# Key loads as one list of rows, scores read every third column

## The chip, the cores and the metric

The kernel runs on one core of one Trainium2 chip. The metric is the device time of one execution in microseconds; the median of several runs is compared. A core has a matrix engine (PE, with its weight loads shown apart as PEld), a vector engine (DVE), a scalar engine (ACT), a general one (POOL) and a queue engine (SP) that issues the transfers. On-chip memory (SBUF) has 128 partitions; PE writes its results to PSUM, eight banks in each partition.

## The reference

Attention of a block of 112 queries over a cache of 512 keys, with the projections before and after it, for 8 batch rows and 32 heads of 192 elements; all inputs are bf16.

```python
B, Sq, D = 8, 112, 640
H, Sk, Dh = 32, 512, 192
q = (x @ wq).reshape(B, Sq, H, Dh).transpose(0, 2, 1, 3)
scores = einsum("bhqd,bhkd->bhqk", q, k_cache) * Dh ** -0.5
p = softmax(scores, axis=-1)
o = einsum("bhqk,bhkd->bhqd", p, v_cache)
out = o.transpose(0, 2, 1, 3).reshape(B, Sq, H * Dh) @ wo
```

## The kernel before, in words

**Tiling.** The heads are taken in two halves of 16. A *group* `t` (0 to 15) is one half of the heads of one batch row: `half, b = divmod(t, 8)`. A *step* `n` (0 to 63) is four heads of a group: `t, s = divmod(n, 4)`. In each step PE computes the scores of four heads, and beside them, for earlier or later steps, the queries' projection (L313), the transposes of the probabilities (L431), the products with the values (L459, L470) and the output projection (L504). DVE takes the scaled scores out of PSUM with their row minimum (`smax`, L396), ACT takes the exponential (`exp`, L401), DVE normalises (`norm`, L405). Two buffers `s_sb` lie between `smax` and `exp`; eight buffers `p_sb` hold probabilities.

**Keys on chip.** TensorE contracts over partitions, so the 192 elements of a key must lie on partitions. Four consecutive keys are 768 elements, six pieces of 128. With `q=4` in `load_k`, a head's keys are 128 rows of 768 elements, and the transposing load (L150) of 16 heads at once sends piece number `3 a + m` of row `r` to column `r` of `kt[t % 2][:, a, m, head]`. For each head and `a` (0 or 1), `m = 0` holds elements 0 to 127 of the even key `4 r + 2 a`; `m = 1` the rest of that key in its first 64 partitions and elements 0 to 63 of the odd key in the others; `m = 2` elements 64 to 191 of the odd key. `kt` has two buffers, one per parity of the group; the load of group `t` waits until the last scores of group `t - 2` are done (`k_done`).

**Score matmuls.** In `scores` each head has an even and an odd product, in two banks of PSUM, of 256 columns each. `Sm` (L368, L370) is the part with 128 rows, `St` (L381, L383) the part with 64 rows, in the upper and lower half of the array. The moving operand is `kt`, `[rows, 2, 128]`: two runs of 128 neighbouring columns. The queries (`qr`, or their shifted copy `qh`) are the weights, 112 columns.

**Order of columns.** A row of scores in PSUM, and in `s_sb`, has the 256 even keys and then the 256 odd ones, in each of them `a` before `r`. The probabilities must go on in four chunks of 128 keys that fit the values' layout (`QJ = [0, 2, 1, 3]`): chunk `(e, a)` holds the keys `4 r + 2 a + e`.

**Group 0** is different: its keys are loaded plainly into `kn` and transposed on PE (`k_transposes`, L281 to L294), which writes the same layout into `kt[0]`.

**Order.** `Plan` holds for each engine a list in program order, written out by hand for the first four steps and for the tail from step 58, and built by a loop between. Each operation waits on semaphores of those named in its `deps`. All loads and stores are on SP's queue, in this order in the middle of the kernel: keys of group `t` (L150), second half of the values of `t - 1` (L165), a piece of the weights `wq` (L198) or `wo` (L208) in some groups, first half of the values of `t`. Five steps near the end (57 to 61) have their probabilities transposed by a transfer (L420) instead of on PE. The final transposes (L592) read `accT` as bf16 with a step of two.

Of the kernel before, what the change touches and what calls it, by code (L numbers as in the profile page):

```python
# [7 lines left out]
ACTF = mybir.ActivationFunctionType  # L8
# [3 lines left out]
class Plan:  # L12
# [7 lines left out]
    def add(self, eng, name, deps, emit, sem=None, inc=1):  # L20
        assert name not in self.ops, name
        self.ops[name] = dict(eng=eng, deps=deps, emit=emit, sem=sem or eng, inc=inc)
# [30 lines left out]
def build_mha_kernel(nc, x, k_cache, v_cache, wq, wo, out):  # L53
    B, SQ, D = x.shape
# [3 lines left out]
    HU = 16  # L58
# [6 lines left out]
    scale = float(DH) ** -0.5  # L65
# [4 lines left out]
    def place(n):  # L70

        return divmod(n, 4)
# [3 lines left out]
    for n in range(NN):  # L76
        t, s = place(n)
# [3 lines left out]
    with ExitStack() as es:  # L81
        def sb(name, shape, dt):
            return es.enter_context(nc.sbuf_tensor(name, shape, dt))
# [3 lines left out]
        accT = sb("accT", [128, B // 2, DC, S2], F32)  # L87
        xT_sb = sb("xT_sb", [128, DC, B * SQ], BF16)
        kt = [sb(f"kt{j}", [128, 2, 3, HU * 128], BF16) for j in range(2)]
        vt = [sb(f"vt{j}", [128, HU // 2, 768], BF16) for j in range(2)]  # L90
        qr = sb("qr", [128, NQ, 3, S2], BF16)
        qh = sb("qh", [128, 2, 2, 4, SQ], BF16)
        s_sb = sb("s_sb", [SQ, NSS, SK], F32)
        p_sb = sb("p_sb", [SQ, 8, SK], BF16)
# [3 lines left out]
        nmx = sb("nmx", [SQ, 8], F32)  # L98
# [3 lines left out]
        ps = es.enter_context(nc.psum_tensor("ps", [128, 8, 512], F32))  # L102
# [24 lines left out]
        def k_done(t, lo, hi):  # L127
            return [("St", step_of[t - 2, s], 3) for s in range(lo // 4, hi // 4)] if t >= 2 else []
# [14 lines left out]
        def load_k(t, lo, hi):  # L143
            half, b = divmod(t, B)
            name = ("K", t, lo)

            def emit(e):
                src = k_cache[b, half * HU + lo:half * HU + hi].rearrange("u (r q) d -> (u r) (q d)", q=4)
                dst = kt[t % 2][:].rearrange("p a m c -> p (a m) c")[:, :, lo * 128:hi * 128]
                return e.dma_start_transpose(dst, src)  # L150
            sem = f"mK{t}_{lo}" if hi - lo < HU else f"mK{t % 2}"
            add("SP", name, k_done(t, lo, hi), emit, sem, 16)
            order["SP"].append(name)
            for s in range(lo // 4, hi // 4):
                k_piece[t, s] = name
# [174 lines left out]
        def q_of(n):  # L330

            t, s = place(n)
            m, bb = divmod(t, 2)
            xs = slice(bb * SQ, (bb + 1) * SQ)
            if m == 1:
                return q1[:, 2 * s:2 * s + 2, :, xs]
            i = q_seq.index((m, 2 * s)) % NQ
            return qr[:, i:i + 2, :, xs]
# [12 lines left out]
        def scores(n):  # L351
            t, s = place(n)
            ktb = kt[t % 2]
            qv = q_of(n)

            def raw(j, c):
                return qv[:, j, c, :]

            def cs(i):
                return slice((4 * s + i) * 128, (4 * s + i + 1) * 128)  # L360

            for j in range(2):
                def emit(e, j=j):
                    for h in range(2):
                        i = 2 * j + h
                        ev, od = (raw(j, 0), qh[:, n % 2, j, 1, :]) if h == 0 else (qh[:, n % 2, j, 2, :], raw(j, 2))
                        hs = slice(h * 256, (h + 1) * 256)
                        e.matmul(ps[0:SQ, 2 * j, hs], ev, ktb[:, :, 0, cs(i)], start=(h == 0), stop=False,  # L368
                                 skip_group_check=True)
                        mm = e.matmul(ps[0:SQ, 2 * j + 1, hs], od, ktb[:, :, 2, cs(i)], start=(h == 0), stop=False,  # L370
                                      skip_group_check=True)
                    return mm
                add("PE", ("Sm", n, j), [("qc", n), ("smax", n - 1, 2 * j), ("smax", n - 1, 2 * j + 1)] +
                    ([("evK", 4 * s + i) for i in range(4)] if t == 0 else [k_piece[t, s]]), emit)
            for i in range(4):
                def emit(e, i=i):
                    j, h = divmod(i, 2)
                    ev, od = ((raw(j, 1)[0:64], qh[64:128, n % 2, j, 0, :]) if h == 0 else
                              (qh[0:64, n % 2, j, 3, :], raw(j, 1)[64:128]))
                    hs = slice(h * 256, (h + 1) * 256)  # L380
                    m1 = e.matmul(ps[0:SQ, 2 * j, hs], ev, ktb[0:64, :, 1, cs(i)], start=False, stop=True,  # L381
                                  skip_group_check=True)
                    m2 = e.matmul(ps[0:SQ, 2 * j + 1, hs], od, ktb[64:128, :, 1, cs(i)], start=False, stop=True,  # L383
                                  skip_group_check=True)
                    return m1, m2
                add("PE", ("St", n, i), [], emit, ("PE", "PE2"))

        def softmax(n):
            for i in range(4):
                j, h = divmod(i, 2)  # L390
                k = (4 * n + i) % 8
                a = (4 * n + i) % NSS
                old = divmod(4 * n + i - NSS, 4)

                def smax(e, j=j, h=h, k=k, a=a):
                    return e.tensor_scalar(s_sb[:, a, :].rearrange("p (e c) -> p e c", e=2),  # L396
                                           ps[0:SQ, 2 * j:2 * j + 2, h * 256:(h + 1) * 256], -scale, None,
                                           op0=ALU.mult, op1=ALU.min, accum_out=nmx[:, k:k + 1])

                def exp(e, k=k, a=a):  # L400
                    return e.activation(p_sb[:, k, :], s_sb[:, a, :], ACTF.Exp, bias=nmx[:, k:k + 1], scale=-1.0,  # L401
                                        accum_out=rsum[:, k:k + 1])

                def norm(e, k=k):
                    return e.tensor_scalar(p_sb[:, k, :], p_sb[:, k, :], rinv[:, k:k + 1], None, op0=ALU.mult)  # L405
                add("DVE", ("smax", n, i), [("St", n, 2 * j + 1), ("exp", *old)], smax)
                add("ACT", ("exp", n, i), [("smax", n, i), ("TD", n - 2) if n - 2 in BY_DMA else ("PT", n - 2, j)], exp)
                add("DVE", ("norm", n, i), [("rc", n, j)], norm)
            for j in range(2):
                k = (4 * n + 2 * j) % 8  # L410

                def rc(e, k=k):
                    return e.reciprocal(rinv[:, k:k + 2], rsum[:, k:k + 2])
                add("DVE", ("rc", n, j), [("exp", n, 2 * j), ("exp", n, 2 * j + 1)], rc)
# [433 lines left out]
def bass_standalone__mha_block_cached__near_ridge_kernel(  # L848
    nc: bass.Bass,
    x: bass.AP,  # L850
    k_cache: bass.AP,
    v_cache: bass.AP,
    wq: bass.AP,
    wo: bass.AP,
    out: bass.AP,
):
    return build_mha_kernel(nc, x, k_cache, v_cache, wq, wo, out)
# [28 lines left out]
```

## Time and profile before

| | |
|---|---|
| median of 3 runs | 456.81 us (456.42 to 457.8) |
| profiled execution: span from first to last instruction | 456.1 us |
| between that span and the median of the runs | 0.7 us |
| mean granted clock of PE | 0.993 |
| exp (L401), 256 times 112x512 f32 | 713 ns each, 182.4 us |
| smax (L396), 256 times | 687 ns each, 167.2 us |
| key loads (L150), 15 transposes | 24.6 us from issue to landing (median) |
| value loads into `vt` (L165), 30 of 1536 KB | 8.6 us from issue to landing (median) |
| bytes moved by transfers | 121.93 MB, 267 GB/s over the span |

The page of the profile gives busy times, and its chain of work that ended last follows the end of the kernel back to what released each step. Times are from one profiled execution. The records of it list no separate execution time beside the span, so the runs' median stands for it here. L followed by a number is a line of the kernel; in a row such as `ps<-kt,qh 128*112 128x256` the output stands first, then the inputs, then rows times columns of the weights and the shape of the moving operand. Busy PE time is modelled from pipelined matmuls; the distance between the starts of neighbouring matmuls is the better measure of their pace.

### The profile page before, as it was taken

The numbers are of one execution on the slowest core, as the hardware profiler recorded it, in microseconds if no ns is written. First come the engines' busy times: TensorE is split into PE (matmuls) and PEld (weight loads), VectorE is DVE, ScalarE is ACT, GpSimd is POOL, SyncE is SP. The second block draws the span as 40 slices with busy tenths as digits, with TensorE's granted clock in tenths as the row PEclk, the third lists the DMA queues.
The fourth block names the chain that finished last, engine by engine and source line by source line (L and its number), as shares of the span: only waits on it lengthen the run. The fifth ranks groups of instructions, "written<-read, shape, count | busy, mean of one in ns | idle before, by whom it ended". The sixth has DMA issues, their size and how long they took to land.

```text
span 456.1 us, 14769 instructions
## 1 busy us (share of the span) xinstructions
PE 432.3 (95%) x6227; PEld 398.1 (87%) x6227; DVE 364.6 (80%) x1160; ACT 334.1 (73%) x782; POOL 0.7 (0%) x6
## 2 busy tenths in 40 slices
PE   5788999999979999999999999997999999999996
PEld 4777888989979899999999999996999999999996
DVE  0577799888868989888888888886688888889971
ACT  3668799867857777877687768776577687767783
POOL 0000000000000000000000000000000000000000
PEclk9999999999999999999999999998899999999999
DMA  8999999999999999999999999999989999999972
GB/s 266 373 363 202 284 244 374 216 314 313 245 317 230 345 230 316 243 293 276 253 319 239 315 228 334 282 235 367 226 225 262 261 213 250 270 225 251 225 204 64
DMA packets 243442, 121.93 MB, mean 267 GB/s; under 512 B 194864, under 2 KB 243376, under 8 KB 243376
## 3 DMA queue, kind: packets, MB, share of 16 engines
q1 hardware_dynamic: 243376, 120.99, 110.0%
q8 instruction: 49, 0.80, 0.7%
q14 instruction: 17, 0.14, 0.1%
HBM read 70.35 MB, written 1.15 MB: 157 GB/s over the span
## 4 chain that ended last, share of the span: by engine, by line
PE 79%; ACT 10%; DMA 6%; DVE 5%; issue 0%; SPq 0%; DVEq 0%
PE ps L504 17%; PE ps L313 16%; PE ps L470 10%; PE ps L431 9%; PE ps L381 7%; ACT p_sb L401 6%; PE ps L459 6%; PE ps L368 6%; PE ps L370 5%; DMA wo_sb<-in_wo_dram 3%; DVE s_sb L396 2%; DMA vt<-in_v_cache_dram 2%; PE ps L543 1%; ACT oT_sb L480 1%; PE ps L567 1%; DVE p_sb L405 1%
## 5 line engine op out<-in xcount | busy, mean ns | idle before, releaser
L401 ACT ACTIVATE p_sb<-s_sb,nmx 112x512 bf16<-112x512 f32 x256 | 182.4, 713 | 83.8 <-DVE s_sb L396 81.8
L396 DVE TENSOR_SCALAR_CACHE_REDUCE s_sb<-ps 112x512 f32<-112x512 f32 x256 | 167.2, 687 | 42.5 <-ACT p_sb L401 20.0
L313 PE MATMUL ps<-xT_sb,wq_sb 128*128 128x224 bf16 x960 | 111.4, 262 | 1.3 <-ACT xT_sb L278 1.3
L504 PE MATMUL ps<-oT_sb,wo_sb 128*128 128x224 bf16 x840 | 97.7, 261 | 3.3 <-DMA wo_sb<-in_wo_dram 3.3
L313 PEld LDWEIGHTS ps<-xT_sb,wq_sb 128*128 128x128 bf16 x960 | 90.2, 99 | 2.8 <-DMA wq_sb<-in_wq_dram 1.1
L405 DVE TENSOR_SCALAR p_sb<-p_sb,rinv 112x512 bf16<-112x512 bf16 x256 | 79.0, 350 | 4.4
L504 PEld LDWEIGHTS ps<-oT_sb,wo_sb 128*128 128x128 bf16 x840 | 78.8, 98 | 3.9 <-DMA wo_sb<-in_wo_dram 3.6
L319 ACT ACTIVATE qr<-ps 128x448 bf16<-128x448 f32 (+1 forms) x112 | 48.9, 441 | 16.1 <-PE ps L313 16.0
L431 PE MATMUL ps<-ident,p_sb 112*128 112x112 bf16 x944 | 57.2, 214 | 1.9 <-ACT oT_sb L480 1.9
L437 ACT ACTIVATE pT_sb<-ps 128x896 bf16<-128x896 bf16 x59 | 53.3, 903 | 4.4 <-PE ps L431 3.7
L431 PEld LDWEIGHTS ps<-ident,p_sb 112*128 112x128 bf16 x944 | 52.0, 99 | 4.1 <-ACT oT_sb L480 4.1
L470 PE MATMUL ps<-pT_sb,vt 128*128 128x112 bf16 x880 | 52.8, 213 | 0.0
L480 ACT ACTIVATE oT_sb<-ps 128x672 bf16<-128x672 f32 x64 | 45.4, 710 | 6.0 <-PE ps L470 6.0
L401 ACT ACTIVATION_READ_ACCUMULATOR p_sb<-s_sb,nmx 112x1 f32 x256 | 48.4, 189 | 0.0
L470 PEld LDWEIGHTS ps<-pT_sb,vt 128*128 128x128 bf16 x880 | 44.1, 98 | 4.3
L437 DVE COPY pT_sb<-ps 128x896 bf16<-128x896 bf16 x59 | 36.4, 616 | 9.1 <-PE ps L431 9.0
L459 PEld LDWEIGHTS ps<-pT_sb,vt 128*64 128x64 bf16 x880 | 24.0, 109 | 14.2 <-issue 9.5
L459 PE MATMUL ps<-pT_sb,vt 128*64 128x112 bf16 x880 | 32.1, 216 | 4.2 <-DVE s_sb L396 2.4
L370 PE MATMUL ps<-kt,qh 128*112 128x256 bf16 x128 | 35.2, 275 | 0.0
L368 PE MATMUL ps<-kt,qh 128*112 128x256 bf16 x128 | 35.1, 274 | 0.0
L368 PE MATMUL ps<-kt,qr 128*112 128x256 bf16 x112 | 31.0, 277 | 3.8 <-DVE qh L346 2.3
L383 PE MATMUL ps<-kt,qh 64*112 64x256 bf16 x128 | 34.0, 291 | 0.0
(70 smaller groups left out, 481.3 us busy)
## 6 DMA issues: line engine op xcount, KB each, us to landing
vt<-in_v_cache_dram SPq DMA_DIRECT2D x30, 1536.0 KB, 8.6
wo_sb<-in_wo_dram SPq DMA_DIRECT2D x4, 1920.0 KB, 13.0
wq_sb<-in_wq_dram SPq DMA_DIRECT2D x7, 960.0 KB, 11.2
wo_sb<-in_k_cache_dram SPq DMA_DIRECT2D x2, 768.0 KB, 10.2
wo_sb<-in_k_cache_dram SPq DMA_DIRECT2D x1, 1536.0 KB, 15.0
wo_sb<-in_v_cache_dram SPq DMA_DIRECT2D x1, 1536.0 KB, 7.8
wq_sb<-in_v_cache_dram SPq DMA_DIRECT2D x1, 1536.0 KB, 8.1
out_dram<-xT_sb SPq DMA_DIRECT2D x8, 140.0 KB, 2.3
```

Source lines behind the costliest of these rows:

```text
L313: mm = e.matmul(ps[:, bank, j * S2:(j + 1) * S2], wq_sb[:, dc, c0:c0 + 128], xT_sb[:, dc, bp * S2:(bp + 1) * S2], start=(dc == 0), stop=(d ...
L368: e.matmul(ps[0:SQ, 2 * j, hs], ev, ktb[:, :, 0, cs(i)], start=(h == 0), stop=False, skip_group_check=True)
L370: mm = e.matmul(ps[0:SQ, 2 * j + 1, hs], od, ktb[:, :, 2, cs(i)], start=(h == 0), stop=False, skip_group_check=True)
L396: return e.tensor_scalar(s_sb[:, a, :].rearrange("p (e c) -> p e c", e=2), ps[0:SQ, 2 * j:2 * j + 2, h * 256:(h + 1) * 256], -scale, None, ...
L401: return e.activation(p_sb[:, k, :], s_sb[:, a, :], ACTF.Exp, bias=nmx[:, k:k + 1], scale=-1.0, accum_out=rsum[:, k:k + 1])
L405: return e.tensor_scalar(p_sb[:, k, :], p_sb[:, k, :], rinv[:, k:k + 1], None, op0=ALU.mult)
L431: mm = e.transpose(psb[:, bank, c:c + SQ], p_sb[:, (4 * n + 2 * j + h) % 8, q * 128:(q + 1) * 128], ident[0:SQ, 0:SQ])
L437: return e.activation(dst, src, ACTF.Copy) if j == 0 else e.tensor_copy(dst, src)
L459: mm = e.matmul(ps[64 * h:64 * h + 64, b0 + j, SQ:2 * SQ], vtb[:, h0 + 2 * j + h, d0:d0 + 64], pT(j, h, q), start=(q == 0), stop=(q == 3))
L470: mm = e.matmul(ps[:, b0 + j, 2 * h * SQ:(2 * h + 1) * SQ], vtb[:, h0 + 2 * j + h, d0:d0 + 128], pT(j, h, q), start=(q == 0), stop=(q == 3))
L480: return e.activation(dst.rearrange("p (j c) s -> p j c s", j=2), ps[:, b0:b0 + 2, 0:3 * SQ].rearrange("p j (c s) -> p j c s", c=3), ACTF. ...
L504: mm = e.matmul(ps[:, o_bank(u, f), j * S2:(j + 1) * S2], wo_sb[:, KU * (u % 2) + k, m * 128:(m + 1) * 128], oT_sb[:, u % NO, k, :], start ...
```

## The change

The key load no longer groups four keys. It reads the 16 heads of a group as one list of 12288 rows of 128 elements, in the order in which they lie in memory, and sends row `i` to column `i` of `kt` seen as one flat row per partition (`ktf`). A head has 768 columns: column `3 w + m` holds piece `m` of the pair of keys `2 w` and `2 w + 1`. The three pieces of a pair mean what `m` meant before, so the same queries meet the same elements, but a score matmul now reads columns `m`, `m + 3`, `m + 6` and so on: 256 columns with a step of three elements. Scores then come in the order of `w`; since `w = 2 r + a`, exp reads its row of `s_sb` with a step of two to put `a` before `r` again, and writes the same order of probabilities as before. Group 0 keeps its layout, so `keys` has a branch for it and exp keeps the plain pattern for `n < 4`. The number of instructions, their waits and their order are as before.

```diff
+        ktf = [k[:].rearrange("p a m c -> p (a m c)") for k in kt]
...
             def emit(e):
-                src = k_cache[b, half * HU + lo:half * HU + hi].rearrange("u (r q) d -> (u r) (q d)", q=4)
-                dst = kt[t % 2][:].rearrange("p a m c -> p (a m) c")[:, :, lo * 128:hi * 128]
-                return e.dma_start_transpose(dst, src)
+                src = k_cache[b, half * HU + lo:half * HU + hi].rearrange("u k d -> (u k d)")
+                return e.dma_start_transpose(ktf[t % 2][:, lo * 768:hi * 768], src.rearrange("(n c) -> n c", c=128))
...
-            def cs(i):
-                return slice((4 * s + i) * 128, (4 * s + i + 1) * 128)
+            def keys(i, m):
+
+                u = 4 * s + i
+                if t == 0:
+                    return ktb[:, :, m, u * 128:(u + 1) * 128]
+                return ktf[t % 2][:, u * 768:(u + 1) * 768].rearrange("p (w m) -> p w m", m=3)[:, :, m]
...
-                        e.matmul(ps[0:SQ, 2 * j, hs], ev, ktb[:, :, 0, cs(i)], start=(h == 0), stop=False,
+                        e.matmul(ps[0:SQ, 2 * j, hs], ev, keys(i, 0), start=(h == 0), stop=False,
                                  skip_group_check=True)
-                        mm = e.matmul(ps[0:SQ, 2 * j + 1, hs], od, ktb[:, :, 2, cs(i)], start=(h == 0), stop=False,
+                        mm = e.matmul(ps[0:SQ, 2 * j + 1, hs], od, keys(i, 2), start=(h == 0), stop=False,
                                       skip_group_check=True)
...
-                    m1 = e.matmul(ps[0:SQ, 2 * j, hs], ev, ktb[0:64, :, 1, cs(i)], start=False, stop=True,
+                    m1 = e.matmul(ps[0:SQ, 2 * j, hs], ev, keys(i, 1)[0:64], start=False, stop=True,
                                   skip_group_check=True)
-                    m2 = e.matmul(ps[0:SQ, 2 * j + 1, hs], od, ktb[64:128, :, 1, cs(i)], start=False, stop=True,
+                    m2 = e.matmul(ps[0:SQ, 2 * j + 1, hs], od, keys(i, 1)[64:128], start=False, stop=True,
                                   skip_group_check=True)
...
                 def exp(e, k=k, a=a):
-                    return e.activation(p_sb[:, k, :], s_sb[:, a, :], ACTF.Exp, bias=nmx[:, k:k + 1], scale=-1.0,
+                    src, dst = s_sb[:, a, :], p_sb[:, k, :]
+                    if n >= 4:
+                        src = src.rearrange("p (e r a) -> p e a r", e=2, a=2)
+                        dst = dst.rearrange("p (e a r) -> p e a r", e=2, a=2)
+                    return e.activation(dst, src, ACTF.Exp, bias=nmx[:, k:k + 1], scale=-1.0,
                                         accum_out=rsum[:, k:k + 1])
```

## The prediction

> **What bounds the kernel now.** First the head of the page and the chain of work that ended last. They name TensorE (PE): 95% busy, 79% of the chain; ScalarE (ACT) holds 10% and transfers 6%.
>
> ```profile
> span 456.1 us, 14769 instructions
> PE 432.3 (95%) x6227; PEld 398.1 (87%) x6227; DVE 364.6 (80%) x1160; ACT 334.1 (73%) x782; POOL 0.7 (0%) x6
> ...
> PE 79%; ACT 10%; DMA 6%; DVE 5%; issue 0%; SPq 0%; DVEq 0%
> ```
>
> A share is a mean over stages, so next the busy time by stretches, each about one group of four steps (one batch row, 16 heads). Columns: stretch, its length, busy time of PE, PEld, DVE, ACT, POOL, granted clock, DMA share, GB/s.
>
> ```profile
> 93.00:145.00 52.00, 48.48 (x705) 45.10 (x702) 41.23 (x130) 36.20 (x85) 0.00 (x0) 1.00 1.21 290
> 171.00:197.00 26.00, 26.00 (x378) 24.26 (x376) 22.63 (x72) 20.11 (x49) 0.00 (x0) 1.00 1.16 281
> 197.00:223.00 26.00, 26.00 (x378) 24.26 (x376) 22.54 (x73) 20.11 (x49) 0.00 (x0) 1.00 1.17 272
> 355.00:381.00 26.00, 26.00 (x378) 24.26 (x376) 22.54 (x73) 20.11 (x49) 0.00 (x0) 1.00 1.03 245
> ```
>
> From about 171 us a group takes 26 us and PE has no gap in it; ACT is idle for 26.0 − 20.1 = 5.9 us. A column that PE streams more slowly there lengthens the kernel by what it costs; work taken from ACT or the transfers buys nothing. The list of waits says how rarely PE waits for a transfer once the loop runs:
>
> ```profile
> PE ps L504 <- DMA wo_sb<-in_wo_dram: 3.3, 1, 3.3
> PE ps L459 <- DMA vt<-in_v_cache_dram: 1.1, 1, 1.1
> ```
>
> That is 4.4 us in two waits, and none is for `kt`. Last, the matmuls that read `kt`, from the timeline of PE:
>
> ```profile
> 185.75 0.27 PE L368 MATMUL ps<-kt,qr 128*112 128x256 bf16 x1
> 185.86 0.27 PE L370 MATMUL ps<-kt,qh 128*112 128x256 bf16 x1
> 185.97 0.27 PE L368 MATMUL ps<-kt,qh 128*112 128x256 bf16 x1
> ...
> 186.87 0.27 PE L381 MATMUL ps<-kt,qh 64*112 64x256 bf16 x1
> 186.87 0.27 PE L383 MATMUL ps<-kt,qr 64*112 64x256 bf16 x1
> 186.98 0.27 PE L381 MATMUL ps<-kt,qr 64*112 64x256 bf16 x1
> ```
>
> Starts are 0.11 us apart (eight from 185.75 to 186.51 give 0.109); the 64-row ones start in pairs. A step has 8 + 4 pairs = 12 slots of 0.109 us, 1.31 us of its 6.5.
>
> **The change part by part.** No instruction is added, removed or moved, and no wait changes: 15 key loads on SP's queue behind the same releases, 16 score matmuls and four exps a step. Three access patterns change, in the 60 steps from n = 4 on.
>
> *The key loads.* Before, the source is 2048 rows of 768 elements, cut into six columns of 128; after, 12288 rows of 128. Both are 2048·6 = 12288 pieces of 256 bytes, 3.15 MB. The trace has the present loads:
>
> ```profile
> L150 SPq DMA_TRANSPOSE kt<-in_k_cache_dram x15: 17199/21185/23057, 24.1 to 391.8; - x15
> ...
> DMA to landing us min/median/max: 19.4/24.6/26.4
> ```
>
> Of the 24.6 us the first part goes to value loads issued ahead on the same queue. Does the order of the source set the pace of the rest? Two stretches answer: 221 to 223 us, where only a key load with its 1536-byte pitch runs, and the densest microsecond of the `p_sb` transposes (L420), whose source is not in HBM at all.
>
> ```profile
> 221.00:223.00 2.00, 2.00 (x40) 1.92 (x35) 1.61 (x5) 1.50 (x5) 0.00 (x0) 1.00 1.28 290
> 434.90:435.90 1.00, 1.00 (x24) 1.00 (x23) 0.73 (x4) 1.00 (x5) 0.00 (x0) 1.00 1.24 284
> ```
>
> 290 and 284 GB/s: two very different sources, one pace. I therefore take the pace as that of the transpose and not of the source, and the key load at no change. Bounds: not above the pace of the plain loads, 374 GB/s in the profile's best slices, which would be 3.15/290 − 3.15/374 = 10.8 − 8.4 = 2.4 us less a load; and a tenth slower, 1.1 us more, as the other end, an estimate of mine.
> What a slower load would cost: keys issued at 176.74 land about 24.6 later, at 201.3, and the first score matmul of their group starts at 205.59. So 4.3 us cover it. A load slower by 1.1 us keeps that cover once, but the queue is full until about 345 us, so delays add up: some ten groups, 11 us of delay less 4.3, at most 7 us.
> What a faster load would buy: only the two waits above, 4.4 us; after them PE's own work is late next.
> [...]
>
> *The score matmuls.* 60 · 12 = 720 slots whose moving operand now steps by 6 bytes instead of 2. No matmul in the trace has a moving operand with a step. The nearest row is on the same engine: the final transposes (L592) load weights with a step of 4 bytes, beside the queries' weights without one.
>
> ```profile
> L592 PEld LDWEIGHTS ps<-ident,accT x40: 128/131/133, 409.7 to 452.5; 128*112 128x112 bf16 x40
> ```
>
> ```profile
> L368 PEld LDWEIGHTS ps<-kt,qh x128: 128/130/217, 14.0 to 437.0; 128*112 128x112 bf16 x128
> ```
>
> 131 against 130 ns for 112 columns: no cost. A farther row is VectorE's add at L522, 391 ns into contiguous f32 and 410 ns into every second bf16, 5% more (the type differs too). A gain is excluded: 256 columns in 0.109 us is also the pace per column of the plain L313 and L504 (0.96 us for ten of 224, 0.43 ns a column). The upper end: a matmul now spans 512 bytes of a partition in 109 ns and will span 1536. No row shows PE spanning SBUF faster than that, so if the span were the limit, the slot would triple: 720 · 0.218 = 157 us. I take no cost, by the row on the same engine; 5% would be 720 · 5.5 ns = 3.9 us.
> [...]
>
> *The exp.* 240 ACTIVATEs read f32 with a step of 8 bytes; what they write stays contiguous, and the maximum and the normalisation are untouched. Mean 713 ns now, four a step. With the 5% of L522 each gets 36 ns more, 16 · 36 = 0.6 us a group, under ACT's 5.9 us of idle time. Without that cover, in the stages before 145 us and the tail, L401 has 6% of the chain, 29 us; 5% of it is 1.4 us. A quicker exp would only lengthen the idle time. I take nothing, keeping 1.4 for the range.
>
> *Sum.* 0 + 0 + 0 against the span of 456.1 us. The median of the runs shown, 456.81, lies 0.7 us above that span. Forecast: 457, its own range 455.5 to 459 (one of the two waits shorter; the exp's 1.4 us).
>
> **The rivals.**
> 1. *The strided stream is slower on PE.* Mechanism: PE fetches stretches of SBUF and uses a third of each, so the slot grows. It decides from 2 ns a slot on (720 · 2 ns = 1.4 us), since nothing waits beside it. At half again, 720 · 0.0545 = 39 us; some 10% of it falls beside ACT's part of the chain: 457 + 36 = 493. At double, 457 + 67 to 78 = 524 to 535. At the 5% row, 461. For it: the span argument above, and that no moving operand with a step was ever shown. Against it: L592. Chance 0.30: 0.06 small, 0.14 around half again, 0.10 double or more.
> 2. *The contiguous source is faster.* Key loads near the plain loads' 8.4 us instead of 10.8: the queue gets ahead and both waits go: 457 − 4.4 = 452.5. Against it: 290 and 284 GB/s from unlike sources. For it: that no contiguous source is shown. Chance 0.20. [...]
> 3. *The exp reads at half pace.* The step from 224 to 448 elements at L319 (352 to 528 ns) is 0.79 ns an element, so 512 of them are 0.40 us. Twice that adds 16 · 0.40 = 6.4 us a group: ACT at 26.5 us passes PE's 26.0, 0.5 us · 13 groups = 7 us, and 13 us in the stages where L401 is on the chain: 464 to 477. Chance 0.08.
> 4. *The key loads get slower or land late*: up to 7 us, 459 to 464. Chance 0.09.
>
> That the change does not do what it says is hardly possible: the patterns are in the text of the diff.
>
> **How the numbers follow.** About 0.3%, 1.4 us, is what a measurement of this kernel can tell from no change. The forecast has the chance 0.33, the largest of a single case: 0.24 within 1.4 us, 0.06 slower by the exp's or a slot's remainder, 0.03 faster. Faster: 0.20 + 0.03 = 0.23. Slower: 0.30 + 0.08 + 0.08 + 0.06 = 0.52. The same: 0.24 and 0.01 of rival 4 = 0.25. So slower is likelier than not, though spread over several prices, and no change is the likeliest single price. The range must reach rival 2 below and the half-again case above: 451.5 to 500. Left out are the doubled slot (0.10) and some 0.05 at either end.
>
> **What would show it.** Starts of L368 and L370 0.109 us apart and 26.00 of 26.00 in a group: no cost on PE; a wider spacing is rival 1, and the spacing times 720 its size. `kt` landing near 24.6 us and 290 GB/s in a stretch of key loads alone: the pace is the transpose's; 350 or more is rival 2, and the wait of L504 for `wo_sb` goes. L401 near 713 ns: the step of two is free. The prediction is wrong if PE waits for `kt`, or if a slot changes by more than 2 ns.

## The result: 7% slower, and the profile after

The changed kernel takes 490.32 us (median of 4 runs, 489.76 to 491.03) against 456.75 us of the kernel before: a ratio of 1.0732, with a 95% interval of 1.0682 to 1.0782. The profiled execution took 490.6 us, its span is 488.7.

The head of the page after, and its chain of work that ended last:

```profile
span 488.7 us, 14769 instructions
PE 473.8 (97%) x6227; PEld 407.9 (83%) x6227; DVE 366.6 (75%) x1160; ACT 343.3 (70%) x782; POOL 0.7 (0%) x6
...
PE 91%; ACT 5%; DVE 3%; DMA 1%; issue 0%; DVEq 0%
```

The same 14769 instructions; PE has 91% of the chain where it had 79, and transfers 1% where they had 6. The timeline of PE in a step of the middle (start, duration, line) has the reason:

```profile
196.32 0.33 PE L372 MATMUL ps<-kt,qr 128*112 128x256 bf16 x1
196.49 0.34 PE L374 MATMUL ps<-kt,qh 128*112 128x256 bf16 x1
196.66 0.33 PE L372 MATMUL ps<-kt,qh 128*112 128x256 bf16 x1
...
197.51 0.34 PE L374 MATMUL ps<-kt,qr 128*112 128x256 bf16 x1
```

Seven gaps in 1.19 us: a slot is 0.170 us and was 0.109. Nothing waits in between, as the busy time by stretches shows (stretch, length, PE, PEld, DVE, ACT, POOL, granted clock, DMA share, GB/s; the last of them has a transposing key load by itself):

```profile
171.00:199.00 28.00, 28.00 (x362) 24.17 (x359) 21.92 (x69) 20.08 (x47) 0.00 (x0) 1.00 1.05 250
199.00:227.00 28.00, 28.00 (x364) 24.43 (x360) 22.29 (x72) 20.83 (x48) 0.00 (x0) 1.00 1.05 253
228.00:230.00 2.00, 2.00 (x36) 1.92 (x31) 1.57 (x7) 1.79 (x5) 0.00 (x0) 1.00 1.27 290
```

PE is full, at full clock. A group now takes 29.0 us (step 24 begins at 189.36 us, step 28 at 218.34; before 179.51 and 205.59). The key load alone still moves 290 GB/s. It lands after 20.5 us (median) instead of 24.6, with the queue emptier (a DMA share of 1.05 in a group where it was 1.16 and 1.17), and ACT's exp is 42 ns longer:

```profile
DMA to landing us min/median/max: 19.5/20.5/24.7
```

```profile
L409 ACT ACTIVATE p_sb<-s_sb,nmx 112x512 bf16<-112x512 f32 x256 | 193.0, 755 | 112.5 <-DVE s_sb L400 112.3
```

The list of waits has no wait of the output projection (L512) for `wo_sb` and none of L467 for `vt` any more.

### The profile page after: what moved, and what is told of

Same layout as the page of the kernel before. It is cut to its first block, busy times and chain, and to the rows that moved or that the text cites. A ratio compares the mean times of both kernels' runs of the same rounds, so it can differ in the third digit from the quotient of the medians.

```text
span 488.7 us, 14769 instructions
## 1 busy us (share of the span) xinstructions
PE 473.8 (97%) x6227; PEld 407.9 (83%) x6227; DVE 366.6 (75%) x1160; ACT 343.3 (70%) x782; POOL 0.7 (0%) x6
## 2 busy tenths in 40 slices
DMA packets 243442, 121.93 MB, mean 249 GB/s; under 512 B 194864, under 2 KB 243376, under 8 KB 243376
## 4 chain that ended last, share of the span: by engine, by line
PE 91%; ACT 5%; DVE 3%; DMA 1%; issue 0%; DVEq 0%
PE ps L313 17%; PE ps L512 16%; PE ps L478 11%; PE ps L385 10%; PE ps L439 9%; PE ps L374 9%; PE ps L372 9%; PE ps L467 6%; ACT p_sb L409 3%; PE ps L551 1%; PE ps L575 1%; DVE s_sb L400 1%; DMA oT_sb<-in_x_dram 1%; ACT qr L319 1%; ACT oT_sb L488 1%; PE ps L600 1%
## 5 line engine op out<-in xcount | busy, mean ns | idle before, releaser
L409 ACT ACTIVATE p_sb<-s_sb,nmx 112x512 bf16<-112x512 f32 x256 | 193.0, 755 | 112.5 <-DVE s_sb L400 112.3
L512 PE MATMUL ps<-oT_sb,wo_sb 128*128 128x224 bf16 x840 | 96.6, 259 | 0.0
L512 PEld LDWEIGHTS ps<-oT_sb,wo_sb 128*128 128x128 bf16 x840 | 78.3, 98 | 0.0
L319 ACT ACTIVATE qr<-ps 128x448 bf16<-128x448 f32 (+1 forms) x112 | 49.5, 445 | 15.2 <-PE ps L313 15.0
L409 ACT ACTIVATION_READ_ACCUMULATOR p_sb<-s_sb,nmx 112x1 f32 x256 | 49.6, 194 | 0.0
L387 PE MATMUL ps<-kt,qh 64*112 64x256 bf16 x128 | 44.2, 347 | 0.0
L374 PE MATMUL ps<-kt,qh 128*112 128x256 bf16 x128 | 42.5, 332 | 0.0
L372 PE MATMUL ps<-kt,qh 128*112 128x256 bf16 x128 | 42.2, 329 | 0.0
L385 PE MATMUL ps<-kt,qh 64*112 64x256 bf16 x128 | 41.5, 326 | 0.0
L372 PE MATMUL ps<-kt,qr 128*112 128x256 bf16 x112 | 36.9, 329 | 3.8 <-DVE qh L346 3.4
L385 PE MATMUL ps<-kt,qr 64*112 64x256 bf16 x112 | 38.5, 346 | 0.0
```

The source lines that it names most:

```text
L319: return e.activation(q_home(m, lp)[:, blocks[0]:blocks[0] + n, :], ps[:, bank, 0:n * S2].rearrange("p (c s) -> p c s", c=n), ACTF.Copy)
L372: e.matmul(ps[0:SQ, 2 * j, hs], ev, keys(i, 0), start=(h == 0), stop=False, skip_group_check=True)
L374: mm = e.matmul(ps[0:SQ, 2 * j + 1, hs], od, keys(i, 2), start=(h == 0), stop=False, skip_group_check=True)
L385: m1 = e.matmul(ps[0:SQ, 2 * j, hs], ev, keys(i, 1)[0:64], start=False, stop=True, skip_group_check=True)
L409: return e.activation(dst, src, ACTF.Exp, bias=nmx[:, k:k + 1], scale=-1.0, accum_out=rsum[:, k:k + 1])
L512: mm = e.matmul(ps[:, o_bank(u, f), j * S2:(j + 1) * S2], wo_sb[:, KU * (u % 2) + k, m * 128:(m + 1) * 128], oT_sb[:, u % NO, k, :], start ...
```

## The experiments

The theory after the first comparison: the stepped read on PE is the whole loss. Its rivals: the list load, or the exp, has a part of it.

**The step alone.** The changed kernel with the loads and the exp of before:

```diff
-                src = k_cache[...].rearrange("u k d -> (u k d)")
-                return e.dma_start_transpose(ktf[t % 2][:, lo * 768:hi * 768], src.rearrange("(n c) -> n c", c=128))
+                src = k_cache[...].rearrange("u (r q) d -> (u r) (q d)", q=4)
+                dst = kt[t % 2][:].rearrange("p a m c -> p (a m) c")[:, :, lo * 128:hi * 128]
+                return e.dma_start_transpose(dst, src)
...
-                    src, dst = s_sb[:, a, :], p_sb[:, k, :]
-                    if n >= 4:
-                        src = src.rearrange("p (e r a) -> p e a r", e=2, a=2)
-                        dst = dst.rearrange("p (e a r) -> p e a r", e=2, a=2)
-                    return e.activation(dst, src, ACTF.Exp, bias=nmx[:, k:k + 1], scale=-1.0,
+                    return e.activation(p_sb[:, k, :], s_sb[:, a, :], ACTF.Exp, bias=nmx[:, k:k + 1], scale=-1.0,
```

> Only the score matmuls step by three columns; the key load (six columns of 128) and the exp (plain) are those of before, so the scores meet other elements than the reference's. Theory A, the stepped stream on PE is the whole loss: the slot goes from 0.109 to 0.170 us as in the changed kernel, 60 steps of 12 slots and 0.061 us each give 43.9 us less what waits give back, 488 to 491 us. Theory B, the list load or the exp has a part of it: 3 us or more below the changed kernel, 487 or less.

Measured 489.63 us (489.4 to 489.95), ratio 1.0728 (1.0679 to 1.0778): the loss of the whole change within 0.7 us, which is about what the exp adds (see the exp alone). Its timeline has the same 0.17 us between neighbours:

```profile
196.00 0.33 PE L373 MATMUL ps<-kt,qh 128*112 128x256 bf16 x1
196.17 0.34 PE L375 MATMUL ps<-kt,qr 128*112 128x256 bf16 x1
196.34 0.33 PE L373 MATMUL ps<-kt,qr 128*112 128x256 bf16 x1
```

**The list load alone**, in the kernel before:

```diff
-                src = k_cache[...].rearrange("u (r q) d -> (u r) (q d)", q=4)
-                dst = kt[t % 2][:].rearrange("p a m c -> p (a m) c")[:, :, lo * 128:hi * 128]
-                return e.dma_start_transpose(dst, src)
+                src = k_cache[...].rearrange("u k d -> (u k d)")
+                return e.dma_start_transpose(ktf[t % 2][:, lo * 768:hi * 768], src.rearrange("(n c) -> n c", c=128))
```

> Only the key load reads the list of 12288 rows; matmuls and exp are those of before, so the scores meet other elements than the reference's. Theory A, the pace is that of the transpose: 290 GB/s in a stretch of key loads alone, landing near 24.6 us, 456 to 458 us. Theory B, the list is slower: over 460 us. The rival of the prediction, a contiguous source is faster: 350 GB/s or more and 447 to 453 us.

Measured 456.0 us against 456.53, ratio 0.9991 (0.9959 to 1.0024). Keys land after 24.0 us (median), and two stretches with a key load by itself show the pace:

```profile
194.00:196.00 2.00, 2.00 (x31) 2.00 (x29) 1.61 (x7) 1.94 (x5) 0.00 (x0) 1.00 1.27 290
221.00:223.00 2.00, 2.00 (x29) 2.00 (x27) 1.86 (x7) 2.00 (x6) 0.00 (x0) 1.00 1.28 290
```

A list of neighbouring rows (290 GB/s), rows with a pitch of 1536 bytes (290) and a source on chip (284, both in the prediction's stretches): one pace. The 350 GB/s or more that the rival asks for is not seen in these stretches.

**The exp alone**, in the kernel before:

```diff
-                    return e.activation(p_sb[:, k, :], s_sb[:, a, :], ACTF.Exp, bias=nmx[:, k:k + 1], scale=-1.0,
+                    src, dst = s_sb[:, a, :], p_sb[:, k, :]
+                    if n >= 4:
+                        src = src.rearrange("p (e r a) -> p e a r", e=2, a=2)
+                        dst = dst.rearrange("p (e a r) -> p e a r", e=2, a=2)
+                    return e.activation(dst, src, ACTF.Exp, bias=nmx[:, k:k + 1], scale=-1.0,
```

> Only the exp reads with a step of two from step 4 on; loads and matmuls are those of before, so probabilities meet other values than the reference's. Theory A, the 45 ns that each exp takes longer in the changed kernel lie under ACT's idle time: L401 near 755 ns and 456 to 458 us. Theory B, the softmax ring feels it: 240 times 45 ns is 10.8 us at most, 460 to 467 us.

Measured 456.58 us against 456.53, ratio 0.9996 (0.996 to 1.0033), with L405 at 754 ns. The runs can't tell the 42 ns from no cost, and over most of the kernel they lie under ACT's idle time, 5.9 us a group before. The trace shows a small price where the softmax sets the pace: steps 5 to 8 take 5.62 us each in place of 5.46, and with steps 4 and 9 that is 0.8 us in all. The changed kernel has the same against the step alone: 0.7 us, nearly all of it in steps 4 to 8 and in 12, 18 and 19.

**Rows of 384.** The changed kernel with two keys to a source row, so that the three pieces of a pair go to three regions of `kt`:

```diff
-                src = k_cache[...].rearrange("u k d -> (u k d)")
-                return e.dma_start_transpose(ktf[t % 2][:, lo * 768:hi * 768], src.rearrange("(n c) -> n c", c=128))
+                src = k_cache[...].rearrange("u (w q) d -> (u w) (q d)", q=2)
+                dst = ktf[t % 2].rearrange("p (m c) -> p m c", m=3)[:, :, lo * 256:hi * 256]
+                return e.dma_start_transpose(dst, src)
...
-                return ktf[t % 2][:, u * 768:(u + 1) * 768].rearrange("p (w m) -> p w m", m=3)[:, :, m]
+                return ktf[t % 2][:, m * 4096 + u * 256:m * 4096 + (u + 1) * 256]
```

> The whole computation, with the exp's step of two kept, but the key load reads rows of 384 elements (two keys), so that each of the three pieces fills 256 neighbouring columns and the score matmuls read without a step. Theory A: slot back at 0.109 us, 456 to 458 us. If something else than the step of three slows the matmuls (the flat layout, the order of keys): slot over 0.12 us and over 470 us.

Measured 455.96 us, ratio 0.9981 (0.9955 to 1.0007): no difference from before that the runs can tell, and the slot is back at 0.109 us. Key order, flat layout and the exp's step are those of the change; only the step of the matmuls is gone, and the loss with it. The first theory holds, its rivals fall.

**What a step costs.** The kernel before, with a `keys` function like the change's in which the score matmuls read with another step in each group:

```diff
+                o = u * 512
+                if t in (13, 14):
+                    g = 2 if t == 13 else 4
+                    return ktf[t % 2][:, o:o + 768].rearrange("p (w g) -> p w g", g=3 * g)[:, :, 0:g]
...
+                step = [0, 1, 2, 3, 4, 5, 6, 7, 8, 10, 12, 16, 2][t]
+                if t == 12:
+                    o += 1
+                return ktf[t % 2][:, o:o + 256 * step].rearrange("p (w m) -> p w m", m=step)[:, :, 0]
```

In the groups 13 and 14 it reads two of every six and four of every twelve neighbours.

> Loads and exp are those of before; the score matmuls of group t read columns with a step that depends on t: 1 to 8 for t = 1 to 8, then 10, 12, 16 for t = 9 to 11, 2 from an odd column for t = 12, two neighbours of every six for t = 13, four neighbours of every twelve for t = 14, and the pattern of before for t = 15. The scores so meet other elements than the reference's. The spacing of L372 to L374 in each group is what counts. Theory A, the price is that of each 16-byte stretch touched, 0.170 us over 96 of them or 1.77 ns: 0.109 us at 1, 0.113 at 2, 0.170 at 3, 0.227 at 4, 0.283 at 5, 0.340 at 6, 0.397 at 7, and 0.453 from 8 on without further growth; 0.170 for the twos and fours, which touch as many stretches as a step of 3. Theory B, the price is for each column that has no neighbour: 0.170 at every step from 2 on, 0.14 for the twos, 0.125 for the fours. [...]

The timeline of PE in this kernel, at steps of 2, 4 and 8:

```profile
84.77 0.27 PE L384 MATMUL ps<-kt,qh 128*112 128x256 bf16 x1
...
85.45 0.27 PE L384 MATMUL ps<-kt,accT 128*112 128x256 bf16 x1
...
145.22 0.41 PE L384 MATMUL ps<-kt,qh 128*112 128x256 bf16 x1
...
146.58 0.41 PE L384 MATMUL ps<-kt,qr 128*112 128x256 bf16 x1
...
279.48 0.63 PE L384 MATMUL ps<-kt,qh 128*112 128x256 bf16 x1
...
281.74 0.63 PE L382 MATMUL ps<-kt,qh 128*112 128x256 bf16 x1
```

Six gaps in 0.68 us, six in 1.36 and five in 2.26 give 0.113, 0.227 and 0.452 us. All of them, read in the same way:

| columns read | 16-byte stretches touched | expected by theory A, us | slot, us |
|---|---|---|---|
| step 1 | 32 | 0.109 | 0.109 |
| step 2 (from an even or an odd column) | 64 | 0.113 | 0.113 |
| step 3 | 96 | 0.170 | 0.171 |
| step 4 | 128 | 0.227 | 0.227 |
| step 5 | 160 | 0.283 | 0.283 |
| step 6 | 192 | 0.340 | 0.340 |
| step 7 | 224 | 0.397 | 0.394 |
| steps 8, 10, 12, 16 | 256 | 0.453 | 0.45 to 0.46 |
| two of every six | 96 | 0.170 | 0.171 |
| four of every twelve | 64 | 0.170 | 0.113 |

The expectation miscounted the last row: fours lie at bytes 0 to 7, 24 to 31, 48 to 55 and so on, each within one stretch, so 64 are touched, and 64 · 1.77 = 0.113 us is what came. With that row put right, the price per stretch holds in every row; theory B holds only at a step of 3, from which both theories took their price. That a stretch is 16 bytes is read from the same table: the slot grows up to a step of 8 columns of 2 bytes, 0.45 us, and no further at 10, 12 and 16. In these rows a moving column costs 0.43 ns or its share of 1.77 ns per 16-byte stretch, whichever is more. Two columns used of each stretch, at a step of four, take 0.227 us, and four, at a step of two, take 0.113, still a little over the 0.109 without a step.

**The same for the exp**, whose source is f32, with a step of 2, 4, 8 and 16 in groups 2 to 5 of the kernel before:

```diff
+                    g = [1, 1, 2, 4, 8, 16][n // 4] if n < 24 else 1
+                    src, dst = s_sb[:, a, :], p_sb[:, k, :]
+                    if g > 1:
+                        src = src.rearrange("p (r a) -> p a r", a=g)
+                        dst = dst.rearrange("p (a r) -> p a r", a=g)
...
```

> The kernel before with the exp reading its 512 scores with a step of 2, 4, 8 and 16 elements in groups 2, 3, 4 and 5 and plainly elsewhere, so probabilities meet other values than the reference's. Theory A, the price per 16-byte stretch is PE's, 1.77 ns, with 402 ns of the plain exp's 713 being its stream: 256 stretches at a step of 2 give 453 ns of stream and 764 ns, 512 at 4, 8 and 16 give 906 and 1217 ns. Theory B, the 42 ns are a fixed price of a pattern with one more dimension: about 755 ns at every step.

The exp's row in ACT's groups of this kernel, in one window each inside group 2 (step 2), 3 (step 4) and 4 (step 8):

```profile
L406 ACT ACTIVATE p_sb<-s_sb,nmx 112x512 bf16<-112x512 f32 x8 | 6.0, 754 | 1.6 <-DVE s_sb L396 1.6
...
L406 ACT ACTIVATE p_sb<-s_sb,nmx 112x512 bf16<-112x512 f32 x7 | 8.5, 1224 | 0.4 <-DVE s_sb L396 0.4
...
L406 ACT ACTIVATE p_sb<-s_sb,nmx 112x512 bf16<-112x512 f32 x8 | 9.8, 1225 | 1.8 <-DVE s_sb L396 1.8
```

754, 1224 and 1225 ns where theory A has 764, 1217 and 1217 (some 1170 at 16). At a step of two alone theory B's 755 fits as well; a step of four decides against it. If 402 ns of the plain exp's 713 are its stream, an estimate from L319 (352 and 528 ns for 224 and 448 elements in the kernel before), ACT pays 1.73 ns a stretch at a step of two, 1.78 at four and eight and 1.68 at 16, about PE's price. By the same estimate a contiguous f32 stream is already at 402/128 = 3.1 ns a stretch. As measured, a step of two costs the exp some 42 ns and a step of four 511.

**Can the waits of before go without a slower PE?** The changed kernel lost less than its slots cost, because waits for transfers went away (next section). So the loads of before were cut, the other loads set between the halves:

```diff
+            cut = t < NT - 1
...
-                load_k(t, 0, HU)
+                load_k(t, 0, HU // 2 if cut else HU)
             load_v(t - 1, 8, 16)
...
+            if cut:
+                load_k(t, HU // 2, HU)
```

In a second kernel only three loads are cut:

```diff
-            cut = t < NT - 1
+            cut = t in (3, 4, 11)
```

> The kernel before with each key load from group 3 to 14 cut into two halves of 8 heads, and the second half of the earlier group's values and the piece of weights issued between the halves; the whole computation. Theory A, the three waits of before for transfers (1.1 us at 102, 2.4 at 130, 3.3 at 317, the last followed by half the clock) come from values and weights that queue behind keys not needed yet: they go, 447 to 453 us. Theory B, the queue is simply full until 345 us and the waits move elsewhere: 455 to 459 us.

> As the kernel with all key loads cut, but only those of groups 3, 4 and 11, the ones ahead of the three waits. Theory A: the same waits go, 447 to 453 us, and where cutting costs the transposes something, this one is the quicker of the two. Theory B: 455 to 459 us.

All of 3 to 14 cut: 455.63 us, ratio 0.9973 (0.9946 to 0.9999), a gain of a quarter per cent that hardly clears zero. Steps 12 and 16 shrink from 6.27 and 8.70 us to 5.28 and 6.23, so the late values were the cause there; step 44 still takes 10.24 of 11.94, steps 3 and 32 lose 0.7 and 1.0 us, and steps 60 and 61 lose 2.6 us in the tail. Only three cut: 457.55 us, 1.005 (1.0012 to 1.0087). The three waits are gone, and its list of waits has only 0.5 us for `vt` left; but step 20 now takes 12.17 us in place of 6.41 and step 48 takes 8.75 in place of 6.23, at waits that the profile puts down to DVE. The one in step 20 (timeline of PE of the kernel with three cut, idle time before the instruction in brackets):

```profile
156.33 0.96 PE L462 MATMUL ps<-pT_sb,vt 128*64 128x112 bf16 x16 [3.22 <-DVE rinv L416]
```

It was a wait for values: a piece issued at 147.85 us landed 8.4 us later, at 156.2, just ahead of this matmul.

Two more, to keep the gain and drop the tail's loss, and to send `wo` ahead; the first has only this line,

```diff
-            cut = t < NT - 1
+            cut = 3 <= t <= 11
```

and the second this line and

```diff
+            if t == 11:
+                w_of[t][0](*w_of[t][1:])
             load_v(t - 1, 8, 16)
-            if t in w_of:
+            if t in w_of and t != 11:
```

> As the kernel before with key loads cut into halves, but only for groups 3 to 11, so that the loads of the tail keep their order; the whole computation. With all of 3 to 14 cut, step 60 began 3.7 us earlier than before (415.88 against 419.61) and steps 61 and 62 lost 2.5 us of it to transposes of probabilities queued behind keys. Theory A, the cut as such helps: the 3.7 us stay, 451 to 454 us. Theory B, the loss comes back at another place: 455 to 458 us.

> As the one cut to group 11, with the piece of wo of group 11 issued ahead of the values there instead of behind them; the whole computation. Theory A: the wait of L504 for wo (2.9 us where all loads were cut, and the half clock behind it) goes as well, 447 to 451 us. Theory B: the values are then late instead, at the same place and the same price, 451 to 456 us.

The first takes 461.42 us, ratio 1.0116 (1.0057 to 1.0176), the second 458.54 us, 1.0068 (1.0034 to 1.0102). Both lie above the ranges of both theories. What B says of the mechanism fits, only the price is higher. In the first, steps 47 and 48 take 7.44 and 9.54 us in place of 6.23, and its list of waits has

```profile
PE ps L462 <- DMA vt<-in_v_cache_dram: 5.0, 4, 3.2
```

In the second, with `wo` ahead, the values are 5.4 us late in the same step 44, which takes 13.83 us in place of 11.94:

```profile
PE ps L464 <- DMA vt<-in_v_cache_dram: 5.4, 1, 5.4
```

None of the four orders clearly beats the kernel before; each moved waits to another place. That the queue is full there, so that an order only chooses who is late, fits this, but no kernel with less to load was run to show it.

## Why the prediction was right or wrong

The range held the time and slower was the likeliest direction; the forecast itself, no change, was wrong, and the first rival's half-again case came: 493 against 490.3. By the prediction's own sign, a slot that changes by more than 2 ns, its price was wrong: the slot changed by 61.

*The step that failed* is "I take no cost, by the row on the same engine". Why the row, weights at a step of 4 bytes in 131 ns, did not show the price is an estimate: 112 columns of 4 bytes are 28 stretches, and if a weight load paid the same price, 28 · 1.77 = 50 ns would lie hidden under the 131. A moving operand takes a column every 0.43 ns, so its 96 stretches of 1.77 ns, 170 ns, lie above its 109. The farther argument, that a matmul would have to span 1536 bytes where it spanned 512, was the right one; only its size was too big, since the runs price a span by the stretches touched, and the contiguous read touches 32: at 1.77 ns that is 57 ns of its 109, an estimate, with nearly half of its room unused.

*The size of rival 1.* What the runs show of its mechanism is the price of a stretch, 1.77 ns; how PE fetches one no run shows. The slot rose by 0.061 us (0.0545 was taken for half again), 720 · 0.061 = 43.9 us. The prediction expected 36 of its 39 us to be left at the end; of the 43.9, 33.6 were. That 493 came so near is luck in part: the slot cost 4.7 us more than half again, and some 7 us more than expected was given back. The discount was also put in the wrong place. Apart from the steps around 44, every step from 21 on takes 0.73 us more than the same step before, 12 slots of 0.061, with nothing absorbed; what is given back comes in a few steps. Steps 5 to 9 give back 1.2 us, where the softmax set the pace before, and steps 18 to 20 another 0.5. The rest is waits of the kernel before that are gone. The largest is in step 44; the first score matmuls of steps 44 and 45 in the timeline of PE, after:

```profile
334.32 0.33 PE L372 MATMUL ps<-kt,qr 128*112 128x256 bf16 x1
...
341.28 0.33 PE L372 MATMUL ps<-kt,qr 128*112 128x256 bf16 x1
```

6.96 us, as every such step. Before, the two stood at 309.92 and 321.86, 11.94 us where its kind took 6.24: 5.7 us, though the list of waits said 3.3. The rest is the clock, which was half in the stretch after the wait and some 1.4 us into step 45, which took 8.06 us in place of 7.38 (busy time by stretches, before):

```profile
313.00:317.00 4.00, 0.89 (x10) 0.64 (x7) 2.67 (x9) 3.17 (x9) 0.00 (x0) 0.93 1.06 364
317.00:321.00 4.00, 3.78 (x29) 3.36 (x30) 0.58 (x1) 0.92 (x1) 0.00 (x0) 0.50 1.26 258
```

Steps 12 and 16 give back 1.0 and 2.5 us. So the waits for transfers were worth about 10 us before (1.0, 2.5, 5.7 and 0.7) and not the 4.4 that the prediction read from two rows: it missed the half clock, and a wait of 2.4 us of L459 that the profile lists under DVE and that was one for values. They were issued at 121.93 us and landed 8.3 us later, at 130.2; L459 went on at 130.37, and the wait goes when they are issued earlier.

*The key loads*: right, and shown by the load alone, at 290 GB/s and 456.0 us. That they land earlier after the change comes with the slower PE and not with the list: with the step alone, at the old load, they land after 20.5 us too, and the DMA share of a group is 1.00.

*The exp*: right within what was kept for it. 42 ns instead of the 36 of the 5% case, and 0.7 to 0.8 us where the softmax sets the pace, inside the 1.4 of the range.

*Rivals 2, 3 and 4*: the contiguous source is no faster (290 GB/s), the exp is far from half pace (755 ns against 713), and no key load came late: the list of waits after has none for `kt` from a transfer.

*What would show it*: the spacing of L368 and L370 was named, and it was the decisive row; the other condition, PE waiting for `kt`, never came.

## What to carry to other kernels

Count the 16-byte stretches of a partition that a matmul's moving operand touches: here each costs 1.77 ns against 0.43 ns a bf16 column, so a step of two is nearly free (0.113 against 0.109 us for 256 columns) and a step of three is 1.56 times as long. A row of another operand with a step proves little unless its own stream runs at the same pace: here 112 columns of weights took 131 ns, and as many columns of the moving operand 48. And before a layout is bent to make a transposing load's source contiguous, look whether that load's pace depends on the source at all: here three sources had one (290, 290 and 284 GB/s).

## What the runs showed of the hardware beside that

A wait of 3.3 us of PE cost 5.7 in its step, the difference being a stretch at a granted clock of 0.50. Not every such wait is followed by one: after the 3.2 us that the kernel cut to group 11 waits until 347.33 us, sixteen matmuls of L473 take 0.96 us and the ten of L316 behind them 1.12, as without a wait, while after the 2.9 us until 314.72 in the kernel with 3 to 14 cut a slot takes 0.212 us (five gaps from 318.13 to 319.19).

A PE that the profile shows as never idle was also granted less, at the larger steps. In the kernel with a step for each group the granted clock was 1.00 with steps of 3, 4 and 5 (100 to 192 us), and 0.91 in the group with a step of 6 (192 to 232 us). With steps of 8 and of 10 the busy time by stretches reads

```profile
279.00:328.00 49.00, 49.00 (x377) 31.27 (x375) 22.79 (x73) 20.95 (x48) 0.00 (x0) 0.79 0.49 116
328.00:378.00 50.00, 50.00 (x380) 31.84 (x379) 23.11 (x73) 22.09 (x49) 0.00 (x0) 0.80 0.65 179
```

The price per stretch was the same at half clock. With a step of 4, in a group at 1.00 (128 to 157 us), it is 0.227 us for 128 stretches, 1.77 ns; with a step of 8 the 64-row pairs behind the slots of the table lie at half clock and start as far apart as those slots (timeline of PE, and the granted clock there):

```profile
294.80 0.63 PE L395 MATMUL ps<-kt,qh 64*112 64x256 bf16 x1
...
295.70 0.63 PE L395 MATMUL ps<-kt,qh 64*112 64x256 bf16 x1
```

```profile
294.50:296.00 1.50, 1.50 (x8) 0.44 (x6) 0.41 (x1) 0.00 (x0) 0.00 (x0) 0.50 0.00 0
```

Two gaps in 0.90 us are 0.45 us each, 1.76 ns for each of 256 stretches. Neighbouring columns were slower at half clock: in step 45 of the kernel before, at half clock, a slot took 0.212 us instead of 0.109 (five gaps from 321.86 to 322.92). What the clock counts was not tried.
